# Two batches of an attention chunk issued side by side on TensorE, in a kernel of attention and two gated layers

## The chip, the cores and the metric

The kernel runs on one core of a Trainium2 chip, in one launch. The metric is the device time of an execution in microseconds (us). Three runs of the kernel before took 516.58, 519.93 and 520.37 us; their median is 519.93 us.

## The reference

The inputs are q, k, v of 2 batches, 8 heads, 768 positions and 64 channels, a decay per head (`lam`, 0.97 to 0.99), and the weights of two feed-forward layers. All is fp32.

```python
for b in range(nb):                    # blocks of 64 positions, for every batch and head
    intra = (qb @ kb.T * Dmask) @ vb   # Dmask[i, j] = lam ** (i - j) for i >= j, else 0
    inter = (qb * lam ** (pos + 1)) @ kv_state
    out[b] = intra + inter
    kv_state = lam ** block * kv_state + (kb * lam ** (block - 1 - pos)).T @ vb
x = out as 1536 tokens x 512
x = ((x @ w_a) * (x @ w_b)) @ w_out                       # 512 -> 1536 -> 512
y = max(x @ w1, x @ w2, x @ w3) @ w_out2                  # 512 -> 768 -> 512
```

## The kernel before

**Attention.** The kernel takes chunks of 128 positions instead of 64: 6 chunks of 2 batches, twelve steps n in the list `order`, where step n is batch n % 2 of chunk n // 2. Steps n and n + 1 of an even n are the two batches of one chunk and do not depend on each other; the state of a batch goes from step n to step n + 2.

One step has four groups of eight fp32 matmuls (one per head), each issued as two TensorE instructions, so that a group shows as x16 in the trace:

- S, the scores (`scores`, L396): 64 rows of the array, 128 columns, two at a time. Their product goes to two banks of PSUM; VectorE multiplies each bank with the decay table into `am` (`masked`, L419).
- V, the values (`values`, L435): 128 rows, 64 columns, `am` against v, into the banks `o`.
- E, the queries with the state (L440): 64 rows, 64 columns, four at a time, added into the same banks. The query, times powers of the decay, is made by GpSimd (`side`, L406). There is none for n = 0 and 1.
- U, the update of the state (L447): 128 rows, 64 columns, into a free part of a bank of `o`, with decayed keys from GpSimd (L409). There is none for n = 10 and 11.

At the end of `values`, ScalarE copies both banks of `o` into x (L192), VectorE adds the old, scaled state to the update (L461, called std below; L459 for chunk 0), and ScalarE scales the new state for the next addition in four small instructions (L465, called stt). std of step n comes behind both copies of x of that step.

**The order.** The main loop (L831 on) writes the order of TensorE by hand, as S(n + 2), V(n), E(n), U(n). It also issues the loads of step n + 4 (`aq`: q and k) and n + 3 (`av`: k and v) on SyncE's queue, 512 KB each. From n = 7 it puts one step of the first feed-forward layer behind each step of attention: `plain_group` (L544, matmuls L554, banks `p`), twelve matmuls of 128 x 128 x 384 with operands A11 and A12 (six each; later A21 and A22).

**Other work, placed by a planner.** The class `Pace` (L57) keeps a planned time for each engine. Work of VectorE and ScalarE that no order is written for (converting weights from 64-bit floats, and splitting operands into a high and a low part for matmuls in fp32r) are tasks in a list with ranks. Each call of `pace.pe(cost)` behind a group of matmuls moves TensorE's planned time on by `cost`, and `pump` then emits the next instructions of the tasks as long as their engine's planned time is at most 1.2 us (ScalarE) or 2.0 us (VectorE, GpSimd) ahead of TensorE's. So the costs that are given to `pace.pe` decide where in an engine's queue a task's instruction stands. An engine works through its queue in order.

Two tasks lie in the stretch of this change. The first weights, w0 (load `wr`, L208), are opened at the top of step 3: L225 and L230 on VectorE, L228, L234 and L236 on ScalarE, L238 on VectorE, then `hi` on ScalarE (L192) and `lo` on VectorE (L189). The operands A11, A12, A21 and A22 of the finished x are opened behind step 5: a high part on ScalarE (`x0A`, L192) and a low part on VectorE (`x0A`, L189). The matmuls of `p` need both.

The remaining 450 us are the two feed-forward layers, with Strassen-like products of blocks, all in one order of TensorE behind attention.

Of the kernel before, what the change touches and what calls it, by code (L numbers as in the profile page):

```python
# [15 lines left out]
B, H, S, D = 2, 8, 768, 64  # L16
C = 128
NC = S // C
NP = H // 2
# [145 lines left out]
def decay_attention_gated_mlps(ctx: ExitStack, tc: tile.TileContext, qkv: bass.AP, lam: bass.AP, wup: bass.AP, wdown: bass.AP, out: bass.AP):  # L165
    nc = tc.nc
# [7 lines left out]
    pace = Pace()  # L174

    def slot(name, dt=F32):
        return sp.tile([128, 1536], dt, tag="s", name=name)
# [4 lines left out]
    def bank(name):  # L182
        return pp.tile([128, 512], F32, tag="ps", name=name)
# [7 lines left out]
    def copy(o, a):  # L191
        nc.scalar.activation(out=o, in_=a, func=AF.Copy)  # L192
# [9 lines left out]
    def load_to(n):  # L202
        while state["raw"] <= min(n, len(items) - 1):
            m = state["raw"]
            kind, i = items[m]
            t = wp.tile([128, 1024], I64, tag="r", bufs=2, name=f"wr{m}")
            if kind == "up":
                nc.sync.dma_start(out=t, in_=wup[i])  # L208
            else:
                nc.sync.dma_start(out=t[:, 0:WB], in_=wdown[i])  # L210
            raw[m] = t
            state["raw"] += 1
# [96 lines left out]
    def open_to(what, m):  # L309
        if m < len(items):  # L310
            items_to(m)
            pace.open((what, m))
# [49 lines left out]
    order = [(b, c) for c in range(NC) for b in range(B)]  # L362
    aq, av, am = {}, {}, {}
    sc = {}
    sttab = slot("stt")
    sts = [sttab[:, 768 + 256 * b:1024 + 256 * b] for b in range(B)]
# [3 lines left out]
    def side_of(h):  # L370

        return h % 2 ^ h // 2 % 2

    def rows(h):
        return slice(64 * side_of(h), 64 * side_of(h) + 64)

    def load(n, *which):

        if n >= len(order):
            return  # L380
        b, c = order[n]
        for i in which:
            of, name = ((aq, "aq"), (av, "av"))[i]
            of[n] = slot(f"{name}{n}")
            s = slice(512 if i == 1 and c == NC - 1 else 0, 1024)
            nc.sync.dma_start(out=of[n][:, s], in_=qkv[b * NC + c, i, :, s])

    def scores(n):
        if n >= len(order):
            return  # L390
        q, k = aq[n][:, 0:512], aq[n][:, 512:1024]
        banks = [bank(f"s{n}_{g}") for g in range(2)]
        for h in range(H):
            r, p = rows(h), h // 2
            o = slice(128 * p, 128 * p + 128)
            nc.tensor.matmul(banks[side_of(h)][:, o], k[r, o], q[r, o], start=True, stop=True)  # L396
        sc[n] = banks
        pace.pe(1.1)

    def side(n):  # L400

        if n >= len(order):
            return
        b, c = order[n]
        if c > 0:
            nc.gpsimd.tensor_tensor(out=aq[n][:, 1024:1536], in0=aq[n][:, 0:512], in1=ltab.rearrange("p a i -> p (a i)"), op=ALU.mult)  # L406
            pace.run("POOL", 512)
        if c < NC - 1:
            nc.gpsimd.tensor_tensor(  # L409
                out=av[n][:, 1024:1536].rearrange("p (h d) -> p h d", h=H), in0=av[n][:, 0:512].rearrange("p (h d) -> p h d", h=H),  # L410
                in1=dmask[:, :, :, C - 1:C].rearrange("p g a i -> p (g a) i").to_broadcast([128, H, D]), op=ALU.mult)
            pace.run("POOL", 400)

    def masked(n):
        if n >= len(order):
            return
        am[n] = slot(f"am{n}")
        for g in range(2):
            nc.vector.tensor_tensor(out=am[n][:, 512 * g:512 * g + 512], in0=sc[n][g], in1=dmask[:, g].rearrange("p a i -> p (a i)"), op=ALU.mult)  # L419
            pace.run("DVE", 512)  # L420
        sc.pop(n)

    def values(n):
        b, c = order[n]
        v, kd, qs = av[n][:, 512:1024], av[n][:, 1024:1536], aq[n][:, 1024:1536]
        ps = [bank(f"o{n}_{s}") for s in range(2)]

        def place(h):
            r, p = 64 * (h % 2), h // 2
            return ps[p % 2][r:r + 64, 128 * (p // 2):128 * (p // 2) + 128]  # L430

        for h in range(H):
            p = h // 2
            o = 512 * side_of(h) + 128 * p
            nc.tensor.matmul(place(h), v[:, 64 * h:64 * h + 64], am[n][:, o:o + 128], start=p < 2, stop=False, skip_group_check=True)  # L435
        pace.pe(1.1)
        if c > 0:
            for h in range(H):
                p = h // 2
                nc.tensor.matmul(place(h), sts[b][rows(h), 64 * p:64 * p + 64], qs[rows(h), 128 * p:128 * p + 128], start=False, stop=False, skip_group_check=True)  # L440
            pace.pe(0.65)
        kv = ps[1][:, 256:512]
        if c < NC - 1:
            for h in range(H):
                p = h // 2
                o = 256 * side_of(h) + 64 * p
                nc.tensor.matmul(kv[rows(h), 64 * p:64 * p + 64], kd[:, o:o + 64], v[:, 64 * h:64 * h + 64], start=False, stop=p == NP - 1, skip_group_check=True)  # L447
            pace.pe(0.65)
        j, r = c // 3, c % 3
        if r == 0:  # L450
            xa[j, b] = slot(f"x{j}{b}").rearrange("p (a i) -> p a i", a=KD)
        for s in range(2):
            copy(xa[j, b][:, s:KD:2, C * r:C * r + C], ps[s][:, 0:256].rearrange("p (a i) -> p a i", a=2))
            pace.run("ACT", 256)
        if c < NC - 1:
            src = kv.rearrange("p (a e) -> p a e", a=NP)
            std = sts[b].rearrange("p (a e) -> p a e", a=NP)
            if c == 0:
                nc.vector.tensor_copy(std, src)  # L459
            else:  # L460
                nc.vector.tensor_tensor(out=std, in0=src, in1=stt[b], op=ALU.add)  # L461
            pace.run("DVE", 256)
            if c < NC - 2:
                for p in range(NP):
                    nc.scalar.activation(out=stt[b][:, p], in_=std[:, p], func=AF.Copy, scale=ltab[:, p, C - 1:C])  # L465
                    pace.run("ACT", 64)
# [264 lines left out]
    with tc.manual_schedule():  # L731
# [8 lines left out]
        ps = bank("warm_ps")  # L740
# [90 lines left out]
        for n in range(len(order)):  # L831
            load(n + 4, 0)
            load(n + 3, 1)
            if n in (0, 3):
                load_to(n // 3)
            if n in (3, 6):
                open_to("conv", n // 3 - 1)
                open_to("split", n // 3 - 1)
            if n == 9:
                load_to(NPLAIN + 1)  # L840
                open_to("conv", NPLAIN)
            if n == 0:
                values(n)
            scores(n + 2)
            side(n + 2)
            masked(n + 2)
            if n > 0:
                values(n)
            if n % 6 == 5:
                j = n // 6  # L850
                xo[j] = Operands([xa[j, b] for b in range(B)], f"x{j}", Operands.PLAIN)
                for i in range(8):
                    pace.open((f"x{j}", i))
            if n == 10:
                pace.open(("x0", "sums"))
            if n > 6:
                next(layer1)
# [107 lines left out]
```

## Time and profile before

| what | value |
|---|---|
| runs, us | 516.58, 519.93, 520.37 |
| profiled execution: span from first to last instruction, us | 517.8 |
| profiled execution: time around the span | not given on the page |
| TensorE (PE) busy | 504.9 us, 98% |
| VectorE (DVE) busy | 369.6 us, 71% |
| ScalarE (ACT) busy | 284.2 us, 55% |
| GpSimd (POOL) busy | 53.5 us, 10% |
| DMA, share of 16 engines in the 40 slices | 7 to 9 tenths in the first 13 us, 9 and over up to about 45 us in most slices, then 0 to 4 |

The span is shorter than the median of the runs by 2.1 us and longer than the fastest of them. Shares of the whole span say little about attention: it fills the first 65 us, and there TensorE, the transfers, VectorE and ScalarE all have idle time in turn. The rows below are from that stretch.

### The profile page before, as it was taken

The numbers are of one execution on the slowest core, as the hardware profiler recorded it, in microseconds if no ns is written. First come the engines' busy times: TensorE is split into PE (matmuls) and PEld (weight loads), VectorE is DVE, ScalarE is ACT, GpSimd is POOL, SyncE is SP. The second block draws the span as 40 slices with busy tenths as digits, with TensorE's granted clock in tenths as the row PEclk, the third lists the DMA queues.
The fourth block names the chain that finished last, engine by engine and source line by source line (L and its number), as shares of the span: only waits on it lengthen the run. The fifth ranks groups of instructions, "written<-read, shape, count | busy, mean of one in ns | idle before, by whom it ended". The sixth has DMA issues, their size and how long they took to land.

```text
span 517.8 us, 7790 instructions
## 1 busy us (share of the span) xinstructions
PE 504.9 (98%) x3175; PEld 467.8 (90%) x3175; DVE 369.6 (71%) x550; ACT 284.2 (55%) x447; POOL 53.5 (10%) x46
## 2 busy tenths in 40 slices
PE   6898999999999999999999999999999999999997
PEld 3787899999999999998888888899999999998886
DVE  2578777886777777779966079599997989887000
ACT  1377644655554555478865185555665566556211
POOL 0576000020222112221000000000000000000000
PEclk9899999999999999999999999999999999999999
DMA  7994400122222210133423020202012211120311
GB/s 243 399 418 183 163 1 13 69 81 82 83 81 83 81 46 20 58 123 105 141 91 152 1 75 7 82 1 75 25 65 82 82 61 62 61 62 0 123 61 62
DMA packets 11731, 47.95 MB, mean 93 GB/s; under 512 B 1192, under 2 KB 2992, under 8 KB 9008
## 3 DMA queue, kind: packets, MB, share of 16 engines
q1 hardware_dynamic: 11696, 47.46, 25.3%
q8 instruction: 25, 0.41, 0.3%
q14 instruction: 10, 0.08, 0.0%
HBM read 44.30 MB, written 3.15 MB: 92 GB/s over the span
## 4 chain that ended last, share of the span: by engine, by line
PE 90%; ACT 3%; DVE 3%; DMA 3%; SPq 1%; issue 0%; ACTq 0%
PE yp L653 19%; PE zu L536 16%; PE zv L536 14%; PE out L707 10%; PE bu L536 8%; PE bv L536 7%; PE p L554 6%; PE xu L536 4%; PE xv L536 3%; DMA aq<-qkv_dram 2%; PE o L435 1%; PE s L396 1%; PE o L440 1%; ACT stt L465 1%; DVE w L238 1%; ACT x0A L192 1%
## 5 line engine op out<-in xcount | busy, mean ns | idle before, releaser
L189 DVE TENSOR_TENSOR lo<-w,hi 128x1024 fp32r<-128x1024 f32 (+1 forms) x40 | 43.8, 1095 | 19.7 <-ACT hi L192 19.6
L585 POOL TENSOR_TENSOR g<-z1u,z6u 128x384 f32<-128x384 f32 x20 | 27.1, 1357 | 166.3 <-DVE z6u L567 111.4
L192 ACT ACTIVATE hi<-w 128x1024 fp32r<-128x1024 f32 (+1 forms) x40 | 38.2, 954 | 10.1 <-DVE w L189 6.3
L653 PE MATMUL yp<-gh,dh 128*128 128x512 f32 x108 | 42.0, 389 | 0.0
L653 PE MATMUL yp<-gl,dh 128*128 128x512 f32 x108 | 42.0, 389 | 0.0
L653 PE MATMUL yp<-gh,dl 128*128 128x512 f32 x108 | 42.0, 389 | 0.0
L189 DVE TENSOR_TENSOR gl<-g,gh 128x512 fp32r<-128x512 f32 x36 | 24.9, 707 | 19.3 <-ACT gh L192 19.3
L189 DVE TENSOR_TENSOR w<-w 128x256 f32<-128x256 f32 (+1 forms) x57 | 31.2, 547 | 1.0
L238 DVE TENSOR_TENSOR w<-w,ws 128x1024 f32<-128x1024 f32 x21 | 26.3, 1255 | 7.5 <-ACT w L236 7.5
L230 DVE SCALAR_TENSOR_TENSOR w<-wr,w 128x1024 int32<-128x1024 int32 (+1 forms) x26 | 30.3, 1167 | 0.2
L192 ACT ACTIVATE z7u<-zu 128x384 f32<-128x384 f32 x20 | 9.8, 491 | 34.2 <-PE zu L536 34.2
L236 ACT ACTIVATE w<-w 128x1024 f32<-128x1024 f32 (+1 forms) x26 | 26.4, 1014 | 0.2 <-DVE w L230 0.2
L696 DVE COPY ob<-out 128x256 f32<-128x256 f32 x1 | 0.4, 423 | 36.3 <-PE out L707 36.3
L228 ACT ACTIVATE ws<-wr,bias 128x1024 f32<-128x1024 f32 x21 | 26.0, 1240 | 0.0
L192 ACT ACTIVATE gh<-g 128x512 fp32r<-128x512 f32 x36 | 21.4, 621 | 7.9 <-PE yp L653 7.9
L234 ACT ACTIVATE ws<-ws,bias 128x1024 f32<-128x1024 f32 x21 | 24.2, 1152 | 0.2
L653 PEld LDWEIGHTS yp<-gh,dl 128*128 128x128 f32 x108 | 20.3, 188 | 4.2
L653 PEld LDWEIGHTS yp<-gh,dh 128*128 128x128 f32 x108 | 20.3, 188 | 4.2
L653 PEld LDWEIGHTS yp<-gl,dh 128*128 128x128 f32 x108 | 20.3, 188 | 4.2
L192 ACT ACTIVATE ob<-out 128x512 f32<-128x512 f32 (+1 forms) x12 | 7.0, 580 | 28.6 <-PE out L707 28.2
L419 DVE TENSOR_TENSOR am<-s,tables 128x512 f32<-128x512 f32 x24 | 15.2, 682 | 10.3 <-DMA tables<-tab_d 8.1
L536 PE MATMUL zu<-x0S,hi 128*128 128x384 f32 x80 | 20.4, 335 | 0.0
(201 smaller groups left out, 1490.2 us busy)
## 6 DMA issues: line engine op xcount, KB each, us to landing
wr<-wup_dram SPq DMA_DIRECT2D x21, 1024.0 KB, 4.8
wr<-wdown_dram SPq DMA_DIRECT2D x12, 768.0 KB, 4.3
aq<-qkv_dram SPq DMA_DIRECT2D x12, 512.0 KB, 10.9
av<-qkv_dram SPq DMA_DIRECT2D x10, 512.0 KB, 10.9
out_dram<-ob SPq DMA_DIRECT2D x11, 256.0 KB, 2.0
tables<-tab_d SPq DMA_DIRECT2D x1, 512.0 KB, 6.6
av<-qkv_dram SPq DMA_DIRECT2D x2, 256.0 KB, 9.2
tables<-tab_d SPq DMA_DIRECT2D x2, 128.0 KB, 7.8
```

Source lines behind the costliest of these rows:

```text
L189: (nc.vector if e == "DVE" else nc.gpsimd).tensor_tensor(out=o, in0=a, in1=b, op=op)
L192: nc.scalar.activation(out=o, in_=a, func=AF.Copy)
L228: nc.scalar.activation(out=sign, in_=high.bitcast(F32), func=AF.Identity, bias=bias[:, 0:1])
L230: nc.vector.scalar_tensor_tensor(out=w, in0=low, scalar=29, in1=w, op0=ALU.logical_shift_right, op1=ALU.bitwise_or)
L234: nc.scalar.activation(out=sign, in_=sign, func=AF.Sign, bias=bias[:, 1:2])
L236: nc.scalar.activation(out=f, in_=f, func=AF.Abs)
L238: nc.vector.tensor_tensor(out=f, in0=f, in1=sign, op=ALU.mult)
L536: nc.tensor.matmul(ps, w, x, start=p in FIRST and i == 0, stop=i == len(todo) - 1, skip_group_check=p not in FIRST)
L554: nc.tensor.matmul(ps, w[:, 128 * k:128 * k + 128], x[:, k], start=m == 0, stop=m == 11)
L585: nc.gpsimd.tensor_tensor(out=ga[g.n][:, tokens(g.j, 0)], in0=g.z[1], in1=g.z[6], op=ALU.mult)
L653: nc.tensor.matmul(ps[e], w[:, cols], g, start=k == 0 and m == 0, stop=k == K1 - 1 and m == 2)
L707: nc.tensor.matmul(ps, a[:, o:o + 128], w[:, s], start=k == 0 and n == 0, stop=k == K2 - 1 and n == 2)
```

## The change

Steps 0 and 1 keep their own order, though step 1 now issues V and U ahead of S(3). From n = 2, an even step issues S(n + 2), S(n + 3), then E(n), E(n + 1), then V(n) and U(n); an odd step issues V and U alone. E now comes ahead of V, in a function of its own (`earlier`), which also takes the banks `o`; the flags that mark the first matmul into a bank move with it. The masks and GpSimd's products of steps n + 2 and n + 3 are issued in the even step. The planned costs of groups change: E 0.65 to 0.55, V 1.1 to 0.95, U 0.65 to 0.5 us. The loads stay where they are.

```diff
+    def earlier(n):
+        b, c = order[n]
+        ob[n] = [bank(f"o{n}_{s}") for s in range(2)]
+        if c == 0:
+            return
+        qs = aq[n][:, 1024:1536]
+        for h in range(H):
+            p = h // 2
+            nc.tensor.matmul(place(n, h), sts[b][rows(h), 64 * p:64 * p + 64], qs[rows(h), 128 * p:128 * p + 128], start=p < 2, stop=False, skip_group_check=True)
+        pace.pe(0.55)
+
     def values(n):
...
-            nc.tensor.matmul(place(h), v[:, 64 * h:64 * h + 64], am[n][:, o:o + 128], start=p < 2, stop=False, skip_group_check=True)
-        pace.pe(1.1)
-        if c > 0:
-            for h in range(H):
-                p = h // 2
-                nc.tensor.matmul(place(h), sts[b][rows(h), 64 * p:64 * p + 64], qs[rows(h), 128 * p:128 * p + 128], start=False, stop=False, skip_group_check=True)
-            pace.pe(0.65)
+            nc.tensor.matmul(place(n, h), v[:, 64 * h:64 * h + 64], am[n][:, o:o + 128], start=c == 0 and p < 2, stop=c == NC - 1 and p == NP - 1, skip_group_check=True)
+        pace.pe(0.95)
...
-            pace.pe(0.65)
+            pace.pe(0.5)
...
-            if n == 0:
+            if n < 2:
+                earlier(n)
                 values(n)
-            scores(n + 2)
-            side(n + 2)
-            masked(n + 2)
-            if n > 0:
+                scores(n + 2)
+                side(n + 2)
+                masked(n + 2)
+            elif n % 2 == 0:
+                for i in (n + 2, n + 3):
+                    scores(i)
+                    side(i)
+                    masked(i)
+                for i in (n, n + 1):
+                    earlier(i)
+                values(n)
+            else:
                 values(n)
```

## Rows read from the trace of the kernel before

**Rows 1.** Granted clock in 40 slices, tenths; busy time, PE PEld DVE ACT POOL, clock
```profile
PEclk9899999999999999999999999999999999999999
...
60.00:510.00 450.00, 449.87 (x2417) 423.42 (x2418) 329.99 (x480) 253.30 (x378) 27.13 (x20) 1.00 0.19 67
```

**Rows 2.** Timeline of TensorE: start, duration, [idle before <-releaser]
```profile
18.72 1.09 PE L435 MATMUL o<-am,av 128*64 128x128 f32 x16
19.65 0.64 PE L447 MATMUL o<-av 128*64 128x64 f32 x16
...
29.15 1.16 PE L396 MATMUL s<-aq 64*128 64x128 f32 x16
30.24 1.09 PE L435 MATMUL o<-am,av 128*64 128x128 f32 x16
31.27 0.67 PE L440 MATMUL o<-aq,stt 64*64 64x128 f32 x16
31.86 0.69 PE L447 MATMUL o<-av 128*64 128x64 f32 x16
32.48 1.16 PE L396 MATMUL s<-aq 64*128 64x128 f32 x16
```

**Rows 3.** Timeline of TensorE, where it waits or resumes
```profile
21.09 1.16 PE L396 MATMUL s<-aq 64*128 64x128 f32 x16 [0.81 <-DMA aq<-qkv_dram]
...
23.81 0.69 PE L447 MATMUL o<-av 128*64 128x64 f32 x16
25.82 1.16 PE L396 MATMUL s<-aq 64*128 64x128 f32 x16 [1.33 <-ACT stt L465]
...
42.47 0.62 PE L554 MATMUL p<-x0A,hi 128*128 128x384 f32 x2
...
45.98 0.44 PE L554 MATMUL p<-x0A,hi 128*128 128x384 f32 x1 [2.02 <-DVE x0A L189]
```

**Rows 4.** SyncE's timeline and DMA issues: the load of aq for step 5
```profile
14.51 0.33 SPq L386 DMA_DIRECT2D aq<-qkv_dram  x1
...
aq<-qkv_dram SPq DMA_DIRECT2D x1, 512.0 KB, 11.2
```

**Rows 5.** Timeline of VectorE: std of step 2, parts of w0, A12, a plain sum
```profile
24.96 0.42 DVE L461 TENSOR_TENSOR stt<-o,stt 128x256 f32<-128x256 f32 x1 [1.36 <-ACT x L192]
...
32.20 1.90 DVE L238 TENSOR_TENSOR w<-w,ws 128x1024 f32<-128x1024 f32 x1 [0.54 <-ACT w L236]
36.51 1.22 DVE L189 TENSOR_TENSOR lo<-w,hi 128x1024 fp32r<-128x1024 f32 x1 [0.88 <-ACT hi L192]
...
44.20 1.72 DVE L189 TENSOR_TENSOR x0A<-x,x0A 128x768 fp32r<-128x768 f32 x1
...
58.98 0.95 DVE L189 TENSOR_TENSOR x0s<-x 128x768 f32<-128x768 f32 x1
```

**Rows 6.** Timeline of ScalarE: stt of step 2, parts of w0, copies of x, A11 to A22
```profile
25.42 1.06 ACT L465 ACTIVATE stt<-stt,tables 128x64 f32<-128x64 f32 x4 [0.49 <-DVE stt L461]
26.39 1.28 ACT L228 ACTIVATE ws<-wr,bias 128x1024 f32<-128x1024 f32 x1
27.76 1.15 ACT L234 ACTIVATE ws<-ws,bias 128x1024 f32<-128x1024 f32 x1
...
31.12 1.04 ACT L236 ACTIVATE w<-w 128x1024 f32<-128x1024 f32 x1
...
35.43 1.04 ACT L192 ACTIVATE hi<-w 128x1024 fp32r<-128x1024 f32 x1
36.38 0.63 ACT L192 ACTIVATE x<-o 128x256 f32<-128x256 f32 x2
...
39.07 3.03 ACT L192 ACTIVATE x0A<-x 128x768 fp32r<-128x768 f32 x4
```

**Rows 7.** TensorE's wait ahead of V(0), and the clock behind it (stretch 14.0 to 17.4)
```profile
13.08 0.43 PE L435 MATMUL o<-am,av 128*64 128x128 f32 x2 [2.52 <-DVE am L419]
...
14.00:17.40 3.40, 3.40 (x41) 3.28 (x38) 1.24 (x3) 1.02 (x4) 1.37 (x2) 0.50 1.01 383
```

More of the change, by code (lines that the diff above doesn't have):

```diff
@@ L421, in masked, with place @@
         sc.pop(n)
+    ob = {}
+    def place(n, h):
+        r, p = 64 * (h % 2), h // 2
+        return ob[n][p % 2][r:r + 64, 128 * (p // 2):128 * (p // 2) + 128]
+    def earlier(n):
[8 more added lines that the diff above has]
+        pace.pe(0.55)
     def values(n):
         b, c = order[n]
[L425 to L430, printed above, removed]
+        v, kd = av[n][:, 512:1024], av[n][:, 1024:1536]
+        ps = ob[n]
         for h in range(H):
```

## The prediction

> **What bounds the kernel now.** I read the busy time by stretches first. From 60 to 510 us TensorE is busy 449.87 of 450 us, at the full clock [rows 1], so whatever TensorE reaches late at 60 us comes out late at the end, us for us, and nothing behind attention can win it back. The question is therefore when the first products of the layer (`p`) run, and how much attention work is left then.
>
> TensorE's own order over time shows the rest. Where it is not held up, a step costs 32.48 - 29.15 = 3.33 us: S 1.09, V 1.03, E 0.59, U 0.62 [rows 2]. But it is held up twice. S(4) and S(5) wait [rows 3]: S(4) for its load; S(5) is put down to stt of step 2, whose first part ended at about 25.8, but its own load was issued at 14.51 and took 11.2 us [rows 4], so it landed at 25.7 and is the later fact on any reading. And `p` does its six matmuls with A11 from 42.47, then stands 2.02 us for A12 until 45.98 [rows 3].
>
> The chain of waits runs from step 2 to that point not over TensorE but to and fro between ScalarE and VectorE: copies of x, std, stt, the parts of w0, `hi`, `lo`, the operands A [rows 5, 6]. Two in-order queues that wait for each other are what ends last there.
>
> **TensorE's side: less time per pair.** Between groups of different shape the engine empties: E to U to the next S costs more than the matmuls' own spacing. The one place without that is chunk 0, where U follows V in the same shape of array: V takes 19.65 - 18.72 = 0.93 us there against 1.03 [rows 2]. So 0.10 us goes for leaving a shape. U behind V lasts 0.64 us, behind E 0.69 [rows 2]: 0.05 for entering one. For S, which loads twice as many columns, I take 0.10, an estimate from that row. Per pair of steps the new order has S S, E E, V U V U, three changes instead of eight. S S saves one leaving and one entering, 0.20; E E 0.15; V U V U three, 0.45: 0.8 us per pair, 6.65 to 5.85. If nothing were saved the term is 0; the bound above is 0.2 for each of five, 1.0. I take 0.8, as V's row shows half of it.
>
> Steps 2 to 7 lie before `p`, where TensorE does not set the end, so their savings are worth nothing by themselves. Steps 8 to 11 lie among products of `p`, back to back: eleven changes instead of sixteen, five by 0.15: **-0.8 us** on the path, bounds 0 and -1.0.
>
> **S(5) in front of step 2.** The new order puts S(5) right behind S(4), and TensorE is in order. S(5) cannot start before 25.82, its load; the loads and their queue on SyncE are unchanged. E(2), E(3), V(2), U(2) were done in that gap before; now they stand behind it: 25.82 + 1.09 (S) + 1.02 (E E) + 0.92 (V) puts U(2) at 28.85 instead of 23.81 [rows 3], and std(2), 1.15 us behind the start of its U as before, at 30.0 instead of 24.96 [rows 5]. TensorE nearly makes that up by the faster pairs: it could end U(7) near 43 where `p` began at 42.47. The other two engines do not: their chain starts 5 us later.
>
> **The queues of VectorE and ScalarE.** I followed the planner's arithmetic (its rates, leads and the costs at each call) through both orders. For the kernel before it gives VectorE's order as the rows have it. For the new one it gives: w0 is opened at step 3, which no longer begins with a group S, so its first instruction stands behind std(2), and L228 behind stt(3). Later, `lo` of w0 lands between std(6) and std(7), and the low parts of A11 and A12 behind std(7): both masks of a pair now come first and push VectorE's planned time ahead, and the smaller costs keep TensorE's back.
>
> Step by step, with the durations of [rows 5, 6]: std(2) to 30.4; stt 1.06, copies of step 3 to 32.0; std(3) to 32.4; stt to 33.5; L228, L234, L236 in a row, 1.28 + 1.15 + 1.04, to 36.9; L238 1.22 (by `lo`, the same shape; its 1.90 contains a wait) to 38.1; std(4) to 38.5; stt to 39.6; copies 0.63, std(5) to 40.6; stt to 41.7; high part of A11 0.84 to 42.4; `hi` of w0 1.04 to 43.4; A12 and A21 1.5 to 44.9; copies of step 6 to 45.4; std(6) to 45.9; `lo` 1.22, with 0.2 for GpSimd's turn, to 47.3; std(7), behind stt(6) and its copies, to 48.0; A11's low part 0.95 to 48.9; A12's to 49.8. `p` starts at 48.9 and is at A12 at 49.9. TensorE itself is held at E(7) by std(5) until 40.6 and ends U(7) at 44. Worked in the same way, the order before reaches A12 at 46.5 where the row has 45.98 [rows 3], so I compare like with like: **+3.4 us**. For the bounds: the row itself instead of the working gives +3.9; if `lo` and A11 went ahead of std(6), 2 us less, +1.4.
>
> GpSimd keeps its order of products, and E(n + 1), moved forward, needs its query at 33 and 40 us, and GpSimd makes it two steps ahead: nothing. The pair holds all eight banks of `o` and S; E(5) takes banks that std(3) frees at 32.4, before 33.2: nothing. E(11) follows U(9) with twelve products and E(10) between them, and a std comes 1.15 us behind the start of its U: nothing; if that cover went, E(11) would wait about 1 us.
>
> **TensorE's clock.** It idles about 44 to 48.9, nearly 5 us, and 22.3 to 25.8, 3.5 us. Before, an idle stretch of 2.52 us ahead of V(0) was followed by 3.4 us at 0.50 of the clock, the 1.2 GHz level [rows 7]; the waits of 1.33 and 2.02 [rows 3] lie in slices at the full clock [rows 1]. At half the clock 3.4 us hold 1.7 us of work. For the long gap I take most of it, **+1.4**, as a part of the slow stretch may fall into the gap (0 to 1.7). For the first gap, half a chance of 1.0: **+0.5** (0 to 1.7); it delays U(2) and with it the whole chain.
>
> The Trainium skill (TensorE: Matmul & The Clock Gate, HAM oscillation — how this bites in real kernels) says that gaps for DMA between bursts of matmuls throttle the clock again and that each burst then starts cold. By that both gaps would be paid in full, +3.4 in place of +1.9; the rows agree for 2.52 us and show no fall for 2.02.
>
> **Sum.** 3.4 - 0.8 + 1.4 + 0.5 = +4.5 us. The span goes from 517.8 to 522.3. What lies around it is not shown; the median of the runs stands 2.1 us above it, and I carry that: 519.93 + 4.5 = **524.4 us**, 0.9% slower.
>
> **Rivals.**
> 1. *The queues come out well* (not slower). If VectorE reaches the low parts of A11 and A12 while TensorE is still at V(6) to U(7), the 2.02 us stall goes: `p` runs through from 43.05, at A12 by 44.2 instead of 45.98, and the savings add: -1.8 - 0.8 = -2.6, 517.3 us. It decides on whether A12's low part is done by 44.2. For it: VectorE has idle time (it is 71% busy over the span), and in the old order A12 stood behind std(6). Against it: five us of delay at std(2), and the worked order.
> 2. *Both gaps pay for the clock in full*: 3.4 - 0.8 + 1.7 + 1.7 = +6.0, 525.9 us. For it: both are longer than the 2.52 us that was followed by a fall. Against it: the work of S(4) lies just before the first. It is what the rule of the Trainium skill named above comes to.
> 3. *The clock holds*: +2.6, 522.5 us. Only a 2.02 us wait speaks for it.
> 4. *The groups don't join* (semaphores at each group empty the engine anyway), so the change doesn't do what it says: +0.8 more than the forecast, 525.2. Against it V to U at 18.72 [rows 2].
>
> **How the numbers follow.** The forecast has 0.60, rival 1 0.12, rival 2 0.16, rival 3 0.08, rival 4 0.04. A measurement of this kernel tells about 1% from no change, 5.2 us: below 514.7 is faster, above 525.1 slower. Within the forecast the unknown terms (1.4 to 3.9 on the chain, 0 to 3.4 on the clock) and the spread of the runs, 3.8 us, leave about 0.35 above that line: 0.21; rival 2 gives 0.14, rival 4 0.02, together 0.37. Faster by over 1% needs more than rival 1's whole gain: 0.03. The rest, 0.60, is within 1%. For the range, rival 1 and a little of each end are left out: 520.6, two less than rival 3, to 527.4, rival 2 and the bound of the chain.
>
> **What would show it.** Right: S(5) still at about 25.8 behind a wait of 3.5 us; std(2) near 30; `lo` of w0 behind std(6) on VectorE; the first `p` near 49 behind a wait of 4 to 5 us for `lo` or A11; a stretch at half the clock around 48 to 52; back-to-back S S without a gap; 60 to 510 us still full. Wrong: `p` before 45; S(5) before 25; idle time of TensorE behind 60 us.

## The result, and the profile after

The changed kernel took 525.76 us (median of four runs, 524.38 to 527.84) where the kernel before took 519.81 (516.58 to 520.37, with a fourth run beside the changed one). The ratio is 1.0126, 95% interval [1.0095, 1.0157]: slower by 5.95 us. The forecast was 524.4 us. The profiled executions say the same: a span of 523.5 us against 517.8, 5.7 more.

First the busy time by stretches of the kernel after (columns: length, then busy time and count for PE, PEld, DVE, ACT, POOL, then granted clock, DMA share, GB/s), one stretch to a line:

```profile
22.80:29.50 6.70, 3.33 (x40) 3.14 (x44) 1.20 (x2) 0.00 (x0) 4.08 (x4) 0.50 1.03 421
43.30:46.60 3.30, 3.30 (x44) 2.97 (x46) 2.17 (x4) 3.30 (x8) 2.98 (x3) 0.50 0.53 218
46.70:60.00 13.30, 10.64 (x160) 9.69 (x158) 10.66 (x15) 9.07 (x20) 0.00 (x0) 1.00 0.14 41
65.00:515.00 450.00, 449.87 (x2417) 423.19 (x2414) 331.94 (x482) 253.64 (x377) 27.44 (x20) 1.00 0.19 67
```

The last line answers to [rows 1]: the 450 us of the layers are as full as before, so the loss lies ahead of 65 us. The first two lines are stretches at half the clock, the 1.2 GHz level. TensorE's timeline shows where the time goes:

```profile
26.16 2.08 PE L396 MATMUL s<-aq 64*128 64x128 f32 x16 [5.19 <-DMA aq<-qkv_dram]
...
30.79 0.63 PE L455 MATMUL o<-av 128*64 128x64 f32 x16
...
32.70 2.06 PE L396 MATMUL s<-aq 64*128 64x128 f32 x32
34.68 1.10 PE L438 MATMUL o<-aq,stt 64*64 64x128 f32 x32
...
38.55 2.06 PE L396 MATMUL s<-aq 64*128 64x128 f32 x32
41.14 0.67 PE L438 MATMUL o<-aq,stt 64*64 64x128 f32 x16 [0.54 <-DVE stt L469]
43.23 1.13 PE L438 MATMUL o<-aq,stt 64*64 64x128 f32 x16 [1.42 <-DVE stt L469]
...
48.23 0.44 PE L562 MATMUL p<-x0A,hi 128*128 128x384 f32 x1
51.33 0.44 PE L562 MATMUL p<-x0A,hi 128*128 128x384 f32 x1 [2.66 <-DVE x0A L189]
...
52.30 0.51 PE L562 MATMUL p<-x0A,hi 128*128 128x384 f32 x2
...
53.44 2.06 PE L396 MATMUL s<-aq 64*128 64x128 f32 x32
...
69.38 0.61 PE L562 MATMUL p<-x0A,hi 128*128 128x384 f32 x2
```

Read against [rows 2, 3]: S(5) still starts when its load has landed, 26.16 where it was 25.82, but the wait ahead of it has grown from 1.33 to 5.19 us, since the work of step 2 that filled it now stands behind. U(2) moves from 23.81 to 30.79. S S and E E join into groups of x32, and a pair of steps in full flow takes 38.55 - 32.70 = 5.85 us. `p` runs one matmul at 48.23 and then stands 2.66 us for A11's low part. At 52.30 it comes to A12, and at 52.48 to the second matmul with A12, the first that needs its low part; that one stood at 45.98. S(10), the first group behind these products, starts at 53.44. In the kernel before, TensorE's timeline has S(10) and the products of `p` behind V(11) at

```profile
47.05 1.16 PE L396 MATMUL s<-aq 64*128 64x128 f32 x16
...
63.80 0.62 PE L554 MATMUL p<-x0A,hi 128*128 128x384 f32 x2
```

so S(10) comes 6.39 us later. The products behind V(11) stand at 69.38 after the change.

VectorE's timeline of the kernel after answers to [rows 5]:

```profile
31.90 0.42 DVE L469 TENSOR_TENSOR stt<-o,stt 128x256 f32<-128x256 f32 x1 [2.31 <-ACT x L192]
...
38.89 1.77 DVE L238 TENSOR_TENSOR w<-w,ws 128x1024 f32<-128x1024 f32 x1 [0.34 <-ACT w L236]
...
47.89 0.42 DVE L469 TENSOR_TENSOR stt<-o,stt 128x256 f32<-128x256 f32 x1 [2.42 <-ACT x L192]
48.23 1.22 DVE L189 TENSOR_TENSOR lo<-w,hi 128x1024 fp32r<-128x1024 f32 x1
49.98 0.42 DVE L469 TENSOR_TENSOR stt<-o,stt 128x256 f32<-128x256 f32 x1 [0.54 <-ACT x L192]
50.33 3.55 DVE L189 TENSOR_TENSOR x0A<-x,x0A 128x768 fp32r<-128x768 f32 x4
```

std(2) at 31.90, then L238, std(6) at 47.89, `lo` of w0 behind it, std(7), and the low parts of A11 and A12 last. ScalarE's timeline answers to [rows 6]:

```profile
45.77 1.56 ACT L192 ACTIVATE x0A<-x 128x768 fp32r<-128x768 f32 x2
47.23 0.63 ACT L192 ACTIVATE x<-o 128x256 f32<-128x256 f32 x2
```

The copies of x of step 6 (47.23), for which std(6) waits, stand behind the high parts of A12 and A21. The chain of waits over 18 to 56 us runs from the load to `p` along these instructions (start, duration, what):

```profile
14.40 11.63 DMA aq<-qkv_dram
...
50.33 0.96 DVE x0A L189
```

Its first piece is the load of [rows 4], 11.63 us where it took 11.2; its last are the copies of x of step 7 (49.41), std(7), A11's low part and `p`. S(5) follows the landing of that load: it landed at 26.03 and S(5) started at 26.16, and in the kernel before it landed at 25.69 and S(5) started at 25.82. The same 0.13 us in both speaks for the load there too, and not for stt of step 2, which [rows 3] name.

### The profile page after: what moved, and what is told of

The parts are those of the page before. It is cut to its first block, busy times and chain, and to the rows that moved or that the text cites. A ratio compares the mean times of both kernels' runs of the same rounds, so it can differ in the third digit from the quotient of the medians.

```text
span 523.5 us, 7792 instructions
## 1 busy us (share of the span) xinstructions
PE 504.8 (96%) x3175; PEld 469.9 (90%) x3175; DVE 368.2 (70%) x550; ACT 283.7 (54%) x447; POOL 51.8 (10%) x46
## 4 chain that ended last, share of the span: by engine, by line
PE 89%; DMA 4%; ACT 4%; DVE 2%; issue 1%; SPq 0%; ACTq 0%
PE yp L661 19%; PE zu L544 16%; PE zv L544 13%; PE out L715 9%; PE bu L544 8%; PE bv L544 7%; PE p L562 7%; PE xu L544 4%; PE xv L544 3%; DMA aq<-qkv_dram 2%; DMA tables<-tab_d 1%; PE o L448 1%; ACT stt L473 1%; PE o L438 1%; PE s L396 1%
## 5 line engine op out<-in xcount | busy, mean ns | idle before, releaser
L593 POOL TENSOR_TENSOR g<-z1u,z6u 128x384 f32<-128x384 f32 x20 | 27.4, 1372 | 172.6 <-DVE z6u L575 172.6
L238 DVE TENSOR_TENSOR w<-w,ws 128x1024 f32<-128x1024 f32 x21 | 26.2, 1249 | 8.5 <-ACT w L236 8.5
L192 ACT ACTIVATE x<-o 128x256 f32<-128x256 f32 x24 | 8.2, 374 | 26.4 <-PE o L448 24.6
```

Source lines behind the costliest of these rows:

```text
L238: nc.vector.tensor_tensor(out=f, in0=f, in1=sign, op=ALU.mult)
L593: nc.gpsimd.tensor_tensor(out=ga[g.n][:, tokens(g.j, 0)], in0=g.z[1], in1=g.z[6], op=ALU.mult)
```

## The experiments

Each was timed beside runs of the kernel before on the same chip. Ratios are to those, with 95% intervals; their medians lie between 518.67 and 519.16 us.

**1. S(5) alone moved ahead, in the kernel before.** Its mask and GpSimd's product move with it. Nothing else of the change: no joined steps behind it, old costs.

```diff
-            scores(n + 2)
-            side(n + 2)
-            masked(n + 2)
+            for i in {2: (4, 5), 3: ()}.get(n, (n + 2,)):
+                scores(i)
+                side(i)
+                masked(i)
```

> The kernel before, with one edit: S(5) and its mask stand ahead of V(2), E(2), U(2), all other steps as before. Theory A (the loss is S(5), which waits for its load, in front of step 2, so that the chain std(2), w0, A11, A12 starts late, and the half clock behind the long gap makes it later): std(2) at 29.6 to 31.9 instead of 24.96, p at A12 between 48.5 and 51, 2.3 us slower than before if the clock holds, 4.6 us if it falls behind the gap, as in the kernel after. Theory B (the loss is the pairing itself, its masks and costs, on VectorE's queue at steps 4 to 7): about 0.

525.02 us, 1.0106 [1.0076, 1.0137], 5.9 us slower. On its TensorE timeline S(5) waits as it does after, and `p` comes late:

```profile
24.55 2.08 PE L396 MATMUL s<-aq 64*128 64x128 f32 x16 [3.73 <-DMA aq<-qkv_dram]
...
49.73 0.45 PE L554 MATMUL p<-x0A,hi 128*128 128x384 f32 x1 [1.71 <-DVE x0A L189]
...
50.81 1.56 PE L396 MATMUL s<-aq 64*128 64x128 f32 x16
...
55.69 0.62 PE L554 MATMUL p<-x0A,hi 128*128 128x384 f32 x2
```

The busy time by stretches (granted clock third from the end):

```profile
24.10:30.90 6.80, 6.34 (x70) 5.49 (x72) 1.29 (x2) 0.58 (x2) 4.77 (x5) 0.50 1.02 423
51.40:54.80 3.40, 3.40 (x40) 2.85 (x40) 3.40 (x7) 2.57 (x6) 0.00 (x0) 0.50 0.00 0
```

One group moved past step 2 gives a loss as large as the whole change's. The clock falls twice, at S(5) and behind `p`. The second fall was not in the expectation, which had 4.6 us at most: S(10) comes 3.76 us later than before (50.81 - 47.05), and the group S, V, E, U behind it takes 55.69 - 50.81 = 4.88 us, where before it takes 50.38 - 47.05 = 3.33, 1.55 more.

**2 and 3. Pairs only from step 4, and only from step 8.** Earlier steps keep the order and the costs of the kernel before (`values(n, True)`).

```diff
-            if n < 2:
-                earlier(n)
-                values(n)
+            if n < 4:                      # 8 in the second kernel
+                if n == 0:
+                    values(n, True)
                 scores(n + 2)
...
+                if n > 0:
+                    values(n, True)
```

> The kernel after, with steps 0 to 3 in the order and with the planned costs of before, pairs from step 4. Theory A: no gap of TensorE over 1.5 us ahead of S(5), std(2) at 25; the order of VectorE's queue at steps 4 to 7 still costs something: p at A12 at 47.5 to 48.5, and 1.2 us slower than before with the saved changes of shape of steps 8 to 11 taken off (0 to +1.5). Theory B: nearly the whole loss of 5.9 us stays, with A12 at 51 to 52.

> The kernel after, with steps 0 to 7 as before and only steps 8 to 11 in pairs. Both theories: 0.8 us faster than before (0.6 to 1.0), from the eleven changes of shape in place of sixteen among the products of p; A12 at 46 as before. If the groups did not join: 0.

From 4: 521.8 us, 1.0046 [1.003, 1.0063], 2.65 slower. Step 2 is undisturbed (std(2) at 24.32 us), but `p` waits longer than before on TensorE's timeline:

```profile
46.62 0.69 PE L571 MATMUL p<-x0A,hi 128*128 128x384 f32 x1 [3.48 <-DVE x0A L189]
```

And by stretches, the clock falls around that wait:

```profile
45.10:51.90 6.80, 5.28 (x25) 4.84 (x27) 4.67 (x6) 2.42 (x6) 0.65 (x1) 0.50 0.01 4
```

That fall was not in the expectation. The 5.28 us of work in it lose up to 2.6 us, more than the 1.45 by which the expectation was short. From 8: 518.5 us, 0.9982 [0.996, 1.0005], 0.65 faster, with an interval that touches 1. Its profile has the term by itself, from S(10) to the products of `p` behind V(11) on TensorE's timeline:

```profile
46.83 2.06 PE L396 MATMUL s<-aq 64*128 64x128 f32 x32
...
62.77 0.61 PE L571 MATMUL p<-x0A,hi 128*128 128x384 f32 x2
```

That is 62.77 - 46.83 = 15.94 us, the same as after (69.38 - 53.44), where the kernel before has 63.80 - 47.05 = 16.75. So the joined groups are worth 0.81 us. The pairs of steps 4 to 7 alone thus lose what the runs of the two kernels differ by, 3.3 us, with S(5) in its old place. This and the 5.9 us of S(5) alone come to more than the whole change loses: both hold up the same operands of `p`, and they are no terms of one sum.

**4. The first gap filled**, in the kernel after: 18 matmuls of zeros in bf16 ahead of S(5), into its bank, which S(5) then starts anew.

```diff
+        if n == 5:
+            w = sttab[:, 512:768].bitcast(BF16)
+            for i in range(18):
+                nc.tensor.matmul(banks[0], w[:, 0:128], w, start=True, stop=True)
```

> The kernel after, with 18 matmuls of zeros (bf16, 128 x 512) in the bank of S(5) ahead of S(5), in the gap in which TensorE waits for its load. Nothing else changes, and the result of S(5) overwrites them. Theory A with the clock: no stretch at 0.5 behind 20 us, std(2) at 30 to 30.3 instead of 31.9, 1.6 to 2.2 us faster than the kernel after, that is 3.5 to 4.3 us slower than before. If the clock's fall is hidden by other waits: as the kernel after, 5.9 us slower.

524.24 us, 1.0095 [1.0065, 1.0126], 5.1 slower: between the two expectations (3.5 to 4.3, and 5.9). TensorE's timeline has the filling and what follows:

```profile
20.44 4.06 PE L396 MATMUL s<-stt 128*128 128x512 bf16 x17
25.60 1.16 PE L400 MATMUL s<-aq 64*128 64x128 f32 x16 [1.10 <-DMA aq<-qkv_dram]
...
48.66 0.45 PE L566 MATMUL p<-x0A,hi 128*128 128x384 f32 x1 [4.12 <-DVE x0A L189]
```

The two stretches on either side of 49.3 us:

```profile
16.00:49.30 33.30, 26.70 (x466) 22.19 (x465) 19.91 (x30) 19.57 (x55) 23.86 (x19) 1.00 0.89 362
49.40:52.70 3.30, 3.30 (x15) 2.86 (x15) 2.42 (x4) 0.82 (x3) 0.00 (x0) 0.50 0.00 0
```

S(5) now runs at the full clock, but the gap at `p` is 4.12 instead of 2.66, and the clock falls behind that one. The unfilled kernel does the same in the second profile of it below (4.24, with a fall), so filling the first gap has taken away the fall at S(5) and has left the other.

**5 and 6. Both gaps filled, beside the kernel after again, on one chip.** The second filling stands ahead of the first `p`, in its bank:

```diff
+                if (n, j, b, half) == (0, 0, 0, 0):
+                    w = sttab[:, 512:768].bitcast(BF16)
+                    for i in range(18):
+                        nc.tensor.matmul(pb, w[:, 0:128], w, start=True, stop=True)
```

> The kernel after, with 18 matmuls of zeros ahead of S(5) and 18 more ahead of the first product of p, each in the bank that the next real matmul overwrites; the second lot fits into the wait of about 4 us for A11's low part. With the first gap alone filled, the clock fell in the second (0.5 from 49.35 to 52.76). If that fall costs what a half-speed stretch of 3.4 us holds: no stretch at 0.5 behind 20 us, 1.7 us faster than with one gap filled, 3.2 us slower than before. If the zeros run past 48.7 or the fall was free: as with one gap filled, 4.9 us slower.

> The kernel after, unchanged, beside the one with both gaps filled on the same chip: 5.9 us slower than before (524 to 528 us), with the clock at 0.5 behind at least one of the two gaps.

Filled: 522.81 us, 1.0082 [1.0054, 1.0111], 4.1 slower. Again: 526.33 us, 1.0142 [1.012, 1.0165], 7.7 slower. The difference is 3.5 us. The fillings only keep TensorE at work in the two gaps, and the two profiles put most of it down to the clock: from S(5) to U(2) 30.39 - 25.07 = 5.32 us became 27.54 - 24.49 = 3.05, and the products up to S(10) 3.67 became 2.11, together 3.8 us; another 0.6 is S(5)'s load, which landed that much earlier with the gaps filled. With both gaps filled TensorE's timeline has `p` still waiting for A11:

```profile
42.89 4.06 PE L565 MATMUL p<-stt 128*128 128x512 bf16 x18
...
47.57 0.44 PE L571 MATMUL p<-x0A,hi 128*128 128x384 f32 x1 [0.45 <-DVE x0A L189]
```

And over 20 to 60 us the clock holds:

```profile
20.00:60.00 40.00, 38.23 (x576) 30.97 (x573) 26.22 (x37) 23.12 (x53) 19.59 (x16) 1.00 0.71 283
```

The unchanged kernel, in this second profile of it, waits twice on TensorE's timeline:

```profile
25.07 2.08 PE L396 MATMUL s<-aq 64*128 64x128 f32 x16 [4.72 <-DMA aq<-qkv_dram]
...
30.39 0.63 PE L455 MATMUL o<-av 128*64 128x64 f32 x16
...
50.42 0.65 PE L562 MATMUL p<-x0A,hi 128*128 128x384 f32 x1 [4.24 <-DVE x0A L189]
...
54.09 2.06 PE L396 MATMUL s<-aq 64*128 64x128 f32 x32
```

By stretches, both waits have their fall:

```profile
23.20:30.00 6.80, 4.93 (x58) 4.41 (x60) 1.29 (x2) 0.00 (x0) 4.04 (x5) 0.50 1.04 426
50.50:53.90 3.40, 3.40 (x11) 3.26 (x11) 3.08 (x4) 0.83 (x2) 0.00 (x0) 0.50 0.00 0
```

**7. S(5)'s load earlier**, in the kernel after: the load of w0 is issued at step 2 instead of step 0, behind S(5)'s.

```diff
-            if n in (0, 3):
-                load_to(n // 3)
+            if n in (2, 3):
+                load_to(n - 2)
```

> The kernel after, with the load of w0 (1 MB) issued two steps later, behind aq of step 6, so that aq of step 5 lands about 2.5 us earlier. Theory A (S(5)'s load sets std(2), and with it p): S(5) at 23.3 to 23.7 instead of 26.2, std(2) at 27.4 if the clock holds over a gap of some 3 us, p at A12 near 48.6 to 49.5, 2.2 to 3.6 us faster than the kernel after, 2.3 to 3.7 us slower than before; w0's first instruction has to wait for its load until 29. If the order of VectorE's queue alone set p: as the kernel after, 5.9 us slower than before.

523.72 us, 1.0083 [1.0057, 1.0109], 4.6 slower. S(5) starts at 22.70 and std(2) at 29.05, 2.85 earlier than after; `p` resumes at 47.99, 3.34 earlier, so that it follows S(5), which starts 3.46 earlier. The clock falls twice all the same, at 20.6 to 27.4 and 48.0 to 51.3. The 4.6 us lie between the two expectations (2.3 to 3.7, and 5.9). Waiting for the load is thus one part of the loss and not the whole of it.

**8. The old costs in the new order**: 0.65, 1.1 and 0.65 given to `pace.pe`, instead of 0.55, 0.95 and 0.5.

> The kernel after, with the planned costs of before (E 0.65, V 1.1, U 0.65); TensorE's order is that of after. Followed through the planner, lo of w0 then stands ahead of the masks of steps 8 and 9 and A11's low part ahead of std(6), but A12's still behind std(7), so that p starts about when it did, stops again at A12, and gets through A12 1.8 us later than the kernel after: 7 to 8 us slower than before (with the clock falling as there). If the smaller costs were what hurt: faster than the kernel after by about 2 us, 4 us slower than before.

528.75 us, 1.0175 [1.0133, 1.0217], 9.6 slower, more than the 7 to 8 that were expected. VectorE's timeline shows the order that the costs made:

```profile
47.98 0.94 DVE L189 TENSOR_TENSOR x0A<-x,x0A 128x768 fp32r<-128x768 f32 x1
48.85 0.41 DVE L469 TENSOR_TENSOR stt<-o,stt 128x256 f32<-128x256 f32 x1
50.93 0.42 DVE L469 TENSOR_TENSOR stt<-o,stt 128x256 f32<-128x256 f32 x1 [1.67 <-ACT x L192]
51.27 2.69 DVE L189 TENSOR_TENSOR x0A<-x,x0A 128x768 fp32r<-128x768 f32 x3
```

A11's low part slips in front of std(6), A12's stays behind std(7). `p` now waits three times (1.40, 2.15 and 1.01 us) and the clock is at half from 48.0 to 58.2, over the S S of chunk 5, which takes 3.79 us instead of 2.06. With no instruction changed, the planner's numbers alone stand 3.0 and 2.4 us apart in the medians (525.76 and 526.33 for the kernel after), though the intervals of the ratios overlap.

**9. A12 ahead of std(6), in the kernel before**, to test rival 1's point: TensorE's planned time is put back behind it, so that the order of TensorE stays; the planned times of VectorE and ScalarE do move on.

```diff
+            if n == 6:
+                at = pace.t["PE"]
+                for x in ("A11", "A12"):
+                    xo[0].get(x)
+                pace.t["PE"] = at
```

> The kernel before, with the splits of A11 and A12 placed ahead of step 6's copies and std on ScalarE's and VectorE's queues (A21 and A22 behind them); TensorE's order is that of before. If the 2.02 us wait of p for A12 is a matter of the place of its low part behind std(6) and the masks of step 9: the wait goes (0 to 0.3 us left), 2.0 us faster than before, up to 3.2 by the working from the rows, which puts the old wait 0.5 us too long. If ScalarE or GpSimd's turn sets it: 0 to 0.5 us faster.

517.12 us, 0.9959 [0.9938, 0.9979], 2.0 faster. VectorE's timeline has both low parts ahead of std(6):

```profile
39.64 3.75 DVE L189 TENSOR_TENSOR x0A<-x,x0A 128x768 fp32r<-128x768 f32 x2 [0.67 <-ACT x0A L192]
43.31 0.41 DVE L461 TENSOR_TENSOR stt<-o,stt 128x256 f32<-128x256 f32 x1
```

On TensorE's timeline `p` runs from 42.13 without a wait up to S(10):

```profile
44.53 1.16 PE L396 MATMUL s<-aq 64*128 64x128 f32 x16
```

S(10) comes at 44.53 instead of 47.05; 0.33 of these 2.52 us is S(5), whose load landed that much earlier (25.49 instead of 25.82).

**10. The same edit with pairs from step 8.**

> The two together: A11 and A12 ahead of std(6), and steps 8 to 11 in pairs with E ahead of V, steps 0 to 7 as before. Theory A: the savings add, since TensorE then runs without a stop from step 6 on: 2.8 us faster than before (2.0 and 0.8; up to 4.0). If E(8) and E(9), now early, wait for std(6) and std(7), which stand later on VectorE: the 0.8 us are lost, 2.0 us faster.

515.84 us, 0.9935 [0.9913, 0.9958], 3.3 faster, beside 2.0 without the pairs: by the medians the two gains add, and this version beats both kernels. Its `p` runs through from 43.14. Its profile, of the slowest of the twelve executions (517.7 us), shows only 0.1 of the 0.8: from S(10) to the products of `p` behind V(11) it takes 62.10 - 45.47 = 16.63 us, where the kernel of experiment 9 takes 61.30 - 44.53 = 16.77. The pair E(8), E(9), which takes 49.85 - 48.82 = 1.03 in the kernel of experiment 3, takes 48.88 - 47.45 = 1.43, as it starts before stt of step 7 has ended (47.84), and `p` waits 0.23 us for a mask. So the second case of the expectation came in part, and that the gains add in full rests on the medians alone.

## Why the prediction was right, and where its sizes were off

The sum was +4.5 us, of 3.4 - 0.8 + 1.4 + 0.5. The profile after, taken apart in the same way:

| term | forecast | profile after | from |
|---|---|---|---|
| chain to A12 and through it to S(10), clock aside | +3.4 | +4.8 | (53.44 - 47.05) - 1.6 |
| clock at S(5) | +0.5 | +1.6 | (30.79 - 26.16) - 3.03 |
| clock at `p` | +1.4 | 0 | 1.00 from 46.7 to 60 |
| changes of shape | -0.8 | -0.8 | 15.94 - 16.75 |
| not named | 0 | +0.1 | from there to the end: (523.5 - 69.38) - (517.8 - 63.80) |
| sum | +4.5 | +5.7 | 523.5 - 517.8 |

The 3.03 is the forecast's own working at the full clock: S 1.09, E E 1.02, V 0.92. The direction and the path came as forecast. That the sum came so near has luck in it: the 1.4 that did not come at `p` in this profile stands against 2.5 that the chain and the clock at S(5) were short.

**S(5) ahead of step 2.** Right as a mechanism, and shown: this group alone makes a loss like the whole change's (experiment 1). U(2) was forecast 5.04 us later from the order alone. It came 6.98 later (30.79 - 23.81): 5.04 from the order, 0.34 from the load, and the rest, 1.6, in a stretch at half the clock.

**The queues.** VectorE's order came out as worked: L225 behind std(2), `lo` of w0 between std(6) and std(7), the low parts behind std(7). From std(2) to A12 the working gave 49.9 - 30.0 = 19.9 us. With both gaps filled it is 48.54 - 28.64 = 19.9; in the profile after 52.30 - 31.90 = 20.4, where L238 took 1.77 us and not the 1.22 that I priced it at (1.23 with both gaps filled). It began at 38.89 beside a product of GpSimd that ran from 38.30 to 39.57; with both gaps filled it began at 35.66, with GpSimd idle. The term was mis-sized by 1.4: 0.34 for the load, 0.5 for L238, 0.5 because I set the new order against a working of the old one that was 0.5 above the row [rows 3], and 0.1 that stays open. The bound by the row itself, +3.9, was the better choice.

**The clock.** This is the step that failed, and in size: "for the first gap, half a chance of 1.0". It cost 1.6 us in the profile after and 30.39 - 25.07 - 3.03 = 2.3 in the second profile of that kernel, over the bound of 1.7. I had put S(4)'s work just before the gap against a fall; both profiles show the fall inside the gap, 26.16 - 22.8 = 3.4 and 25.07 - 23.2 = 1.9 us before S(5) starts. The forecast had read the waits of 1.33 and 2.02 as lying in slices at the full clock; the slice with the first reads 8 [rows 1], but for the stretch of [rows 7] alone, which is the only fall in that trace ahead of 60 us. For the gap at `p` the forecast took 1.4, with TensorE idle from 44 on. The second profile shows it: the eleven matmuls up to S(10) take 54.09 - 50.42 = 3.67 us, where at the full clock they take 53.44 - 51.33 = 2.11, so 1.6. The first profile does not have it there: the clock had fallen earlier, from 43.3, behind waits of 0.54 and 1.42 us, and that cost nothing, since the copies of x of step 6 stood behind A12 and A21 on ScalarE until 47.23 anyway. Those waits, of E(6) and E(7) for std(4) and std(5), and that fall are also why TensorE came to `p` only at 48.23 and stood 2.66 us there, not nearly 5. Both together are about 3.5 us of the time of runs (experiments 5 and 6) against 1.9 in the sum.

By the Trainium skill (TensorE: Matmul & The Clock Gate, HAM oscillation — how this bites in real kernels), a gap for DMA between bursts throttles the clock again and the next burst starts cold. The second profile agrees for its gap for the load, 4.72 us, and shows the same behind 4.24 us of waiting for VectorE; the first agrees for 5.19 and shows no fall behind 2.66.

**Changes of shape.** -0.8 forecast, -0.81 measured, in two kernels. A pair took 5.85 us, the number of the forecast. Rival 4 is out: groups of x32 stand without a gap.

**The rivals.** Rival 2, both gaps in full, gave 525.9; the median is 525.76, so it lies nearer than the forecast. Its parts are only half right: its clock terms of 1.7 each stand beside the second profile's 2.3 and 1.6, its chain was as short as the forecast's. Rival 3, the clock holds, gave 2.6 above before; with the clock held by filling, 4.1 were measured. Rival 1 did not come in the new order, but its point decides as described: with A12 ahead of std(6), the kernel before gains 2.0 us, where the stall was worth 1.8. The same placement in the kernel after was not tried, so how much of the loss it would win back there is open.

**Open.** Runs of one kernel spread by 0.8 to 5.4 us, and S(5) started between 24.49 and 26.49 us in the profiles where it kept its load's place. Whether the landing of the load makes that spread was not tried. With both gaps filled, the four runs' median is 4.1 us above before while the profiled execution, the shortest of them at 521.57, is 2.0 us above in span. Of what is missing, 1.33 is the load: S(5) started at 24.49 there and at 25.82 in the kernel before. At the same start the span would be 3.3 above, an estimate from these rows, and the table's terms without the clock, the 0.34 of the load and the 0.5 of L238 give the same 3.3. What the medians have above that, 0.8, is not explained.

## What to carry to other kernels

When groups of an in-order engine are joined, look at what the moved group waits for: the 0.8 us for five changes of shape were there, but a group that waits for its load took the next state update with it, 5 us, into a stretch in which two other queues end last. Join the groups only where the engine itself is the bound (here from step 8), and elsewhere look at the place of the one late operand in its queue, which was worth 2 us by itself. A wait that TensorE gets is to be priced with the half clock behind it, and filling one wait takes away the fall behind that one and no other.

## What the runs showed of the hardware that was not expected

- Filling the first gap took away the fall at S(5) and not the one at `p`: the clock was at 1.00 until 49.3 us and then at 0.50 for 3.3 us behind the gap at `p`. The unfilled kernel has a fall at `p` in its second profile and none in its first, so it is not shown that the filling brought it about. Filling both held the clock at 1.00 from 20 to 60.
- A fall came at 43.3 us behind waits of 0.54 and 1.42 us, while in the second profile of the same kernel a wait of 1.43 ahead of 42.31 had none behind it. The kernel before shows none behind 2.02 [rows 3], but in experiment 1 the clock fell at 51.4 behind a wait of 1.71 at `p`. The length of the last wait alone did not decide it.
- Ahead of V(0), near the start, a wait of 1.66 to 2.83 us stood beside a fall in nine of the twelve profiles, and in the other three a wait of 1.26 to 1.45 us had none; the forecast's row of 2.52 [rows 7] is one of the nine.
